# Stage B's row maxima, minima and sums move into one PSUM bank; three matmul groups share three banks; all steps in a new order

## The chip, the cores and the metric

The kernel runs on one core of a Trainium2 chip. A core has a matrix engine (PE in the profile, with its weight loads as PEld), a vector engine (DVE), a scalar engine for activations (ACT), a general engine (POOL) and a queue engine (SP) that here only starts transfers. Data is worked on in two on-chip memories: SBUF, and PSUM, into which PE writes its sums and which DVE and ACT can read and write too. This kernel cuts PSUM into eight banks of 128 partitions x 512 fp32 values. The metric is the device time of one execution in microseconds (us).

## The reference

For x with S = 2048 rows of D = 512 values, two branches are computed and mixed row by row. H = 32 heads of 16 columns, F = 1376 hidden columns, all in fp32:

```
q, k, v = x @ wqkv, cut into 32 heads of 16
pq = q @ w_phi (per head);  pk = k @ w_phi
phi(p) = concat(softmax(p), softmax(-p))       # 16 -> 32 features a head
kv = sum over rows of phi(pk)^T v;  z = sum over rows of phi(pk)
a = (phi(pq) kv) / (phi(pq) z + 1e-6) @ wo
h = x @ w1 + b1;  b = (h * tanh(softplus(h))) @ w2     # Mish
g = sigmoid(sum(x * gate_w))
out = g * a + (1 - g) * b
```

## The kernel before

Products are made to fp32 precision from two fp32r parts of each operand (high and low), as high x high + high x low + low x high. Some of the products go by a scheme of seven block products in place of eight; the steps `p1` to `p7` of a step group are these, and `c1`, `c5`, `c6`, `a2`, `a3`, `a7` (`e4` in stage A) are the additions that join them. A step is named stage, block, step: `S0.p6_2` is product 6 of pair 2 in block 0 of stage S.

- Stage A, eight chunks `A0` to `A7` of 256 rows: K and its features (`k0`, `k1`, two 128-row tiles), V and Q (`p1` to `p7`), softmaxes of K (`mx`, `mn`, `d0`, `d1`, `E`, `S`, `rS`, `ml`), products of the features with V in one PSUM bank that stays open for the whole stage (tile `kvp`), and sums of the features. The feature tile `E` (128x1024) is added into an accumulator (`zacc`, `za`) partly by transfers that POOL starts (line 484). Q is written to memory and read back as `pq` tiles of 128 rows.
- Stage S, two blocks `S0`, `S1` of 1024 rows: `x @ w1` for pairs 0 to 4 of hidden columns, into PSUM tiles `up`. ACT copies three of the seven products out (`c`), DVE adds the rest (`a2` line 740, `a3` line 743, `a7` line 746), ACT evaluates Mish (`mA`, `mB`). The weights of the next pair are made ready between: the sums `w1r` on DVE (`su`, lines 687 to 690), high parts on ACT, low parts on POOL (`w1sl`, line 700).
- Stage B, four blocks `B0` to `B3` of 512 rows: `h @ w2` in eleven steps `dn0` to `dn10` into four banks (tiles `down`), with low parts `l` made on POOL (line 824). Beside it each block makes the softmax of four `pq` tiles t = 0 to 3 on DVE: row maxima and minima of the 32 heads (`mx`, `mn`, line 275, 128x32), `E` = pq - mx and mn - pq (`d0`, `d1`, lines 285, 287), exponentials on ACT, sums `Sm` (`S`, line 291, 128x64), their reciprocals (`rS`, line 299), `T` = E * z (line 954), its sums `Dn` (`D`, line 958), the denominator (`m`, line 977: Dn * Sm; `de`, line 962), scale (`sc`, line 966), `E` scaled (`es`, line 302), transposed (`tr`, line 969) and sent through memory into `eT`. From these come `num` (`nu`), its two parts (`oh`, `ol`), `wo` and the output (`fi`).

Stages overlap: S0's first pairs run beside the end of A, the down-projection of `B0` and `B1` beside and behind S0, and so on. The order of all 1224 steps is one text, `RUN`, and every engine keeps its part of it: an instruction that waits holds all that stand behind it on the same engine, the transfers that the engine starts included. Matmuls and ACT instructions are recorded by helpers (lines 118, 138), so all of these have one line.

The eight banks are kept in three pools: `a` with three banks, `dn` with four and `kv` with one. The `kv` bank holds `kvp` in stage A. After `A7.km`, in which it is read for the last time, it serves as a fourth bank for three uses:

```
ps["a"] = psum("up", ("a", "kv")[p % 2])                          # p1 of pairs 1 and 3
po = [psum("num", tag) for tag in (("kv", "a"), ("a", "a"))[h]]
num["wo", t] = ps = psum("wo", ("kv", "a")[t % 2])
```

A new tile in a pool takes the bank whose tile is oldest, and its first matmul waits until the last reader of that tile is done. `mx`, `mn` and `Sm` of stage B are SBUF tiles, two buffers each. In stage A `S` lies in the PSUM tile of K itself (tiles `proj`), and the sources of `d0` and `d1` are PSUM tiles too.

Of the kernel before, what the change touches and what calls it, by code (L numbers as in the profile page):

```python
# [46 lines left out]
    A0.st0 A0.st1 A0.z1 A1.c6 A0.z0 A1.z0 S0.h21 A2.c1 A1.p5 A0.kv A1.c5 A1.S1 A1.rS1 A1.p7 A1.p3 A2.sh A2.sl A3.su A2.mn0 A1.ml1 A1.a7 A2.mx1 A1.st1
    A3.k1 A2.a2 A1.a3 A2.mx0 A2.d10 A2.d00 A3.p1 A2.E0 A2.S0 A3.ldx A2.rS0 A1.z1 S0.wr_0 A2.p6 A2.c6 A2.ldx A2.p5 A2.c5 A2.p7 A1.p4 A2.d01 A2.mn1
    A2.d11 A2.E1 A2.p3 A3.sh S0.wa_0 A2.ml0 A1.st0 A3.mn1 A3.c1 A3.k0 A2.a3 A2.z0 A2.st0 A3.sl A3.p5 A2.a7 A2.p4 A1.e4 A3.xh A2.S1 A3.mx0 A3.mx1
    A3.mn0 A1.kv A3.xl S0.l12 A2.e4 A2.rS1 A2.ml1 A2.kv A3.d00 A3.d10 A3.E0 S0.wb_0 S0.ws_0 A3.p6 A4.p1 A2.z1 A3.d11 A3.S0 A3.rS0 A3.ml0 A2.st1 A2.wx  # L50
    A3.c5 A4.k0 A4.mn0 A3.c6 A4.su A3.p3 A4.d10 A3.a3 A4.c1 A3.p7 A4.sh A4.mx0 S0.h11 A4.d00 A3.a7 A4.k1 A4.E0 A3.st1 A3.d01 A4.mn1 A4.d11 A4.S0 A4.sl
    A3.p2 A3.a2 A4.mx1 A4.p5 A4.p6 A3.z0 A3.E1 A4.xh A4.c6 A4.ldx A3.S1 A3.rS1 A4.p2 A4.p7 A4.d01 A4.c5 A3.ml1 A3.p4 A4.a7 A4.st1 A4.E1 A3.st0 S0.o11
    A4.xl A4.rS0 A4.ml0 A4.p3 A5.su A5.sh A4.a3 A3.z1 S0.t1 A3.e4 B0.lq0 A5.k0 A5.k1 A5.mx0 A4.S1 A4.z0 A4.rS1 A4.ml1 A5.sl S0.h1 S0.o1 A4.z1 S0.o21
    A5.xh A5.p1 A5.c1 A3.kv A5.p5 A5.c5 A4.st0 A4.a2 A5.mn0 A5.p6 A5.mx1 A5.xl A5.d01 S0.wc_0 A5.mn1 A5.d10 A5.d11 A5.d00 A5.E0 A4.p4 A5.S0 A5.rS0
# [8 lines left out]
    B0.gl B0.dn0 B0.cd B0.dn1 S0.mA1_0 S0.ws_1 S0.wc_1 A7.zf B0.d01 S0.wd_1 S0.a2_1 S0.p1_2 S0.p6_1 S0.gh3 S0.mA0_1 B0.E1 B0.hi2 B0.lo2 S0.sB0_0 A7.zs
    A7.zl B1.lq3 S0.ws_2 S0.wc_2 S0.p5_1 S0.p2_2 B0.mx2 B0.d02 S0.c6_1 S0.p7_1 S0.c5_1 S0.p3_1 S0.wr_3 B0.T1 B0.S1 B0.mn2 S0.a7_1 S0.mB1_0 S0.sB1_0
    B0.d12 B0.dn2 S0.wd_2 B0.T0 B0.hi3 B0.D1 B0.lq3 S0.c1_2 S0.p6_2 S0.mB1_1 B0.rS0 B0.E2 B0.D0 S0.wa_3 B0.lo3 S0.sB1_1 S0.a2_2 B0.rS1 B0.m1 B0.mx3
    S0.p4_1 S0.mA1_1 B0.hi4 S0.lg2 S0.c6_2 B0.de1 S0.wr_4 B0.dn3 S0.gl3 S0.wb_3 S0.mA0_2 S0.p5_2 S0.p1_3 S0.lg4 S0.c5_2 S0.a3_1 B1.lq0 S0.gh4 B0.lo4
    B0.rd1 B0.m0 B0.T2 S0.p7_2 S0.p3_2 B0.de0 S0.mB0_1 S0.ws_3 S0.wc_3 S0.wd_3 B0.sc1 S0.p2_3 B0.d03 S0.wa_4 S0.wb_4 B0.dn4 B0.es1 S0.a7_2 S0.c1_3
    S0.p6_3 S0.a3_2 B0.mn3 S0.mB0_2 S0.sB0_1 S0.a2_3 B0.d13 B1.mx3 B0.S2 S0.mB1_2 B0.D2 S0.gh2 B0.hi5 S0.c6_3 S0.mA0_3 B0.E3 S0.p4_2 B0.lo5 S0.p1_4
    S0.p5_3 S0.c5_3 B0.tr1 S0.n12 B0.rd0 B0.ge S0.gl2 B0.dn5 B0.sc0 B1.mx0 S0.ws_4 S0.p7_3 B0.es0 S0.p3_3 S0.mA1_2 S0.sB0_2 S0.a7_3 S0.p4_3 B0.rS2
    B0.hi6 S0.wc_4 B0.tr0 B0.lo6 B0.dn6 S0.mB1_3 S0.sB1_2 S0.wd_4 S0.a3_3 S0.mA1_3 S0.mB0_3 S0.sB0_3 B0.T3 B0.D3 B0.S3 B1.d00 B1.lq1 S0.gl4 B0.rS3  # L70
# [1164 lines left out]
```

## Time and profile before

| | |
|---|---|
| median of three runs | 431.92 us (431.51 to 433.22) |
| the profiled execution | 432.84 us |
| its span, first to last instruction | 431.1 us |
| PE busy | 422.3 us, 98% |
| DVE busy | 369.3 us, 86%, 519 instructions |
| ACT busy | 253.6 us, 59% |
| POOL busy | 263.6 us, 61% |
| mean granted PE clock | 0.996 of full speed |

Busy shares are means over the whole span. In a row of groups stand the line, engine and operation, output <- inputs by name, sizes, the count, and then busy time in us, mean in ns, and the idle time in front of these instructions with what ended it. In a row of the time line stand start and duration in us, and in brackets the idle time in front and what ended it. Names there lack the numbers that tell buffers apart.

### The profile page before, as it was taken

How to read it: one execution, taken by the hardware profiler on the slowest of the kernel's cores; microseconds unless marked ns; L12 is line 12 of the kernel's file. 1: busy time of each engine (PE TensorE's matmuls, PEld its weight loads, DVE VectorE, ACT ScalarE, POOL GpSimd, SP SyncE). 2: the span in 40 equal slices, each digit the busy share in tenths (PEclk: the TensorE clock that was granted, in tenths of full speed). 3: DMA queues.
4: the chain of work that ended last, by engine and by line, in shares of the span. 5: the costliest groups of instructions: out<-in, count | busy, mean ns of one | idle time of the engine just before them, and what ended most of it. 6: DMA issues, size and time to landing. Idle time of an engine off the chain costs nothing. (4 is left out here: it accounts for less than half of the span.)

```text
span 431.1 us, 7558 instructions
## 1 busy us (share of the span) xinstructions
PE 422.3 (98%) x2772; PEld 340.2 (79%) x2772; DVE 369.3 (86%) x519; ACT 253.6 (59%) x373; POOL 263.6 (61%) x186
## 2 busy tenths in 40 slices
PE   8999999999998999899999999999999999999996
PEld 7888888888886877688878687788788887877875
DVE  3899789998998999998999998799989699999512
ACT  3574463646254899768679813467978467851131
POOL 2298868799674966635666494977455627541220
PEclk9999999999999999989999999999999999999999
DMA  7900597675988344433888477833533725555532
GB/s 260 366 34 28 164 273 182 140 179 126 209 171 214 108 134 123 160 109 122 235 249 281 165 239 237 281 91 122 177 119 143 232 73 188 179 199 168 197 121 75
DMA packets 52670, 74.06 MB, mean 172 GB/s; under 512 B 8085, under 2 KB 32149, under 8 KB 52633
## 3 DMA queue, kind: packets, MB, share of 16 engines
q1 hardware_dynamic: 50440, 66.36, 47.9%
q0 software_dynamic: 1904, 6.82, 9.5%
q8 instruction: 22, 0.36, 0.3%
q10 hardware_dynamic: 288, 0.39, 0.3%
q14 instruction: 16, 0.12, 0.1%
HBM read 43.53 MB, written 28.85 MB: 168 GB/s over the span
## 5 line engine op out<-in xcount | busy, mean ns | idle before, releaser
L118 PE MATMUL down<-w2g,h 128*128 128x512 f32 x316 | 98.5, 393 | 0.0
L118 PEld LDWEIGHTS down<-w2g,h 128*128 128x128 f32 x316 | 58.6, 188 | 14.8 <-issue 2.5
L118 PE MATMUL down<-w2g,l 128*128 128x512 f32 x158 | 61.8, 391 | 0.2 <-POOL l L824 0.2
L824 POOL TENSOR_TENSOR l<-act,h 128x512 fp32r<-128x512 f32 (+1 forms) x24 | 32.3, 1345 | 41.2 <-ACT h L138 16.7
L824 POOL TENSOR_TENSOR l<-actb,h 128x512 fp32r<-128x512 f32 x20 | 29.0, 1451 | 38.3 <-ACT h L138 20.7
L138 ACT ACTIVATE E<-E 128x1024 f32<-128x1024 f32 x32 | 33.4, 1057 | 16.5 <-DVE E L285 7.1
L118 PE MATMUL up<-x,w1sh 128*128 128x512 f32 x144 | 39.7, 397 | 2.2 <-DVE act L740 2.1
L118 PE MATMUL wo<-woh,ohl 128*128 128x512 f32 x128 | 40.9, 389 | 0.0
L118 PEld LDWEIGHTS down<-w2g,l 128*128 128x128 f32 x158 | 29.6, 188 | 7.5 <-POOL l L824 1.2
L118 PEld LDWEIGHTS up<-x,w1sh 128*128 128x128 f32 x144 | 26.7, 189 | 9.2 <-DVE act L740 2.5
L700 POOL TENSOR_TENSOR w1sl<-w1r,w1sh 128x1024 fp32r<-128x1024 f32 x9 | 22.2, 2467 | 18.0 <-ACT w1sh L138 17.4
L118 PE MATMUL proj<-tw,sx 128*128 128x512 f32 x126 | 31.5, 394 | 1.5 <-ACT qs L138 1.5
L628 POOL TENSOR_TENSOR x<-xr,x 128x1024 fp32r<-128x1024 f32 x10 | 26.7, 2666 | 3.6 <-ACT x L138 3.6
L118 PEld LDWEIGHTS proj<-tw,sx 128*128 128x128 f32 x126 | 23.3, 188 | 6.9 <-ACT qs L138 1.9
L138 ACT ACT_TABLE_LOAD x22 | 28.2, 1283 | 0.4
L118 PEld LDWEIGHTS wo<-woh,ohl 128*128 128x128 f32 x128 | 24.0, 188 | 5.0
L138 ACT ACTIVATE act<-act,b1s 128x512 f32<-128x512 f32 x30 | 21.4, 719 | 10.9 <-DVE act L740 4.1
L118 PE MATMUL up<-x,w1d 128*128 128x512 f32 x108 | 27.7, 398 | 0.0
L267 POOL TENSOR_TENSOR xl<-xraw,xh 128x512 fp32r<-128x512 f32 x14 | 18.3, 1370 | 15.3 <-ACT xh L138 15.0
L138 ACT ACTIVATE act<-up 128x512 f32<-128x512 f32 x30 | 17.6, 590 | 16.8 <-PE up L118 16.4
L138 ACT ACTIVATE h<-actb 128x512 fp32r<-128x512 f32 x20 | 12.4, 628 | 24.4 <-DMA actb<-ab 18.9
L118 PE MATMUL wo<-wol,ohl 128*128 128x512 f32 x64 | 24.9, 389 | 0.0
(173 smaller groups left out, 1086.4 us busy)
## 6 DMA issues: line engine op xcount, KB each, us to landing
ed<-E SPq DMA_DIRECT2D x16, 512.0 KB, 3.1
eT<-ed SPq DMA_DIRECT2D x64, 128.0 KB, 3.2
za<-E POOLq DMA_DIRECT2D x11, 512.0 KB, 6.8
xr<-in_xT_dram SPq DMA_DIRECT2D x20, 256.0 KB, 4.2
ab<-act SPq DMA_DIRECT2D x20, 256.0 KB, 2.9
actb<-ab SPq DMA_DIRECT2D x20, 256.0 KB, 3.3
pqd<-qs SPq DMA_DIRECT2D x16, 256.0 KB, 5.8
pq<-pqd SPq DMA_DIRECT2D x16, 256.0 KB, 3.6
```

The lines of the kernel that those rows point to most:

```text
L118: return pin(nc.tensor.matmul(*a, **k))
L138: return pin(A_.activation(out_, in_, fn, **k))
L267: pin(eng.tensor_sub(xs[c][1][j], kt(rawx[c], SC)[:, 2 * j : 2 * j + 2, :], f32(xs[c][0][j])))
L628: pin((V if n in LOV else G_).tensor_sub(X[n][:, 1024:], xr[n], f32(X[n][:, :1024])))
L700: pin(G_.tensor_sub(W["sl"], W["r"], f32(W["sh"])))
L824: pin(G_.tensor_sub(U[i]["l"][:n, :], U[i]["a"][:n, :], f32(U[i]["h"][:n, :])))
```

## The change

Behind `A7.km` the `kv` bank becomes one tile `sm` that stays to the end. It is cut into three slots of 160 columns. A stage B softmax tile takes a slot, if one is free, at the first of its `mx` and `mn`, keeps `mx`, `mn`, `Sm` and a new product `m` in it, and gives it back at its `es`; if none is free, it uses SBUF tiles as before. By the order of the steps ten of the sixteen tiles get a slot: t = 2, 3 of B0, t = 0, 2, 3 of B1, t = 1, 2, 3 of B2 and t = 1, 2 of B3. For these, `m` is two multiplications of 128x32, the second into the slot, in place of one of 128x64, which adds ten DVE instructions. `up`, `num` and `wo` take the three `a` banks alone. `RUN` is written anew. The matmuls are the same in number. ACT loads its tables 21 times in the program's order, where it was 23.

```diff
 RUN = """
-    A0.mx0 A0.mx1 A0.xh A0.xl A0.v0 A0.mn1 A0.mn0 A0.fq A0.fh2 S0.l11 A0.d10 A0.tA0 A0.fh1 A0.v1 A0.tA1 A0.tH1 A0.fl1 A0.tB1 A0.tB0 A0.fl2 A1.p1
...
+    A1.ldx A0.mn1 A0.v1 A0.d11 A0.xh A0.mn0 A0.xl A0.ve1 A0.d10 A0.mx1 A0.fq A0.fh0 A0.fh2 A0.tA0 S0.l11 A0.d01 A0.tA1 A0.tH1 A0.mx0 A0.fh3 A0.fl3
 """
...
+    B = {}
+    sm, slots = [], [0, 1, 2]
+
+    def small(d, name, o, n, bufs=2):
+        if "slot" not in d:
+            d["slot"] = None
+            if slots and "km" in B:
+                if not sm:
+                    sm.append(psum("sm", "kv"))
+                d["slot"] = slots.pop(0)
+        if d["slot"] is None:
+            return T([P, n], F32, name, bufs, name)
+        o += 160 * d["slot"]
+        return sm[0][:, o : o + n]
...
-            d[name] = T([P, H], F32, name, 2, name)
+            d[name] = small(d, name, H * (name == "mn"), H) if key[0] == "B" else T([P, H], F32, name, 2, name)
...
-            d["S"] = src()[:, : 2 * H] if key[0] == "A" and key[1] else T([P, 2 * H], F32, "Sm", 2, "Sm")
+            if key[0] == "B":
+                d["S"] = small(d, "Sm", 2 * H, 2 * H)
+            else:
+                d["S"] = src()[:, : 2 * H] if key[1] else T([P, 2 * H], F32, "Sm", 2, "Sm")
...
-                ps["a"] = psum("up", ("a", "kv")[p % 2])
+                ps["a"] = psum("up", "a")
...
+            def dm(d=d):
+                if d["slot"] is None:
+                    d["m"] = d["D"][:, H:]
+                    pin(V.tensor_mul(d["D"], d["D"], d["S"]))
+                    return
+                d["m"] = small(d, "", 4 * H, H)
+                pin(V.tensor_mul(d["D"][:, :H], d["D"][:, :H], d["S"][:, :H]))
+                pin(V.tensor_mul(d["m"], d["D"][:, H:], d["S"][:, H:]))
...
-                pin(V.scalar_tensor_tensor(d["d"], d["D"][:, :H], 1e-6, d["D"][:, H:], op0=ALU.add, op1=ALU.add))
+                pin(V.scalar_tensor_tensor(d["d"], d["D"][:, :H], 1e-6, d["m"], op0=ALU.add, op1=ALU.add))
+
+            def es(d=d):
+                scale_by(d, V)
+                if d["slot"] is not None:
+                    slots.append(d["slot"])
...
-                po = [psum("num", tag) for tag in (("kv", "a"), ("a", "a"))[h]]
+                po = [psum("num", "a") for _ in range(2)]
...
-                num["wo", t] = ps = psum("wo", ("kv", "a")[t % 2])
+                num["wo", t] = ps = psum("wo", "a")
```

New line numbers stand some 15 to 30 higher: lines 285, 287, 291, 302 become 301, 303, 310, 321; 687 to 690 become 706 to 709; 740, 743, 746 become 759, 762, 765; 954, 958, 977 become 971, 975 and 980 to 984.

Three places show the order. The first is PE in block 0 of stage S, between pairs 2 and 3; `w1sh`, `w1sl`, `w1d`, `w1o` are weight parts, the number behind a name tells tiles apart. Before:

```order
L118 MATMUL up_1902<-x_595,w1o_1774 128x512 x6
L118 MATMUL up_1787<-x_1570,w1sh_1850 128x512 x4
...
L118 MATMUL up_1787<-x_1634,w1d_1671 128x512 x6
...
L118 MATMUL down_1825<-w2g_211_1561,l_1984 128x512
L118 MATMUL up_2031<-x_1105,w1sh_1893 128x512 x4
L118 MATMUL up_2031<-x_1105,w1sl_1956 128x512 x2
L118 MATMUL up_2038<-x_960,w1d_1980 128x512 x6
L118 MATMUL up_1861<-x_1570,w1sh_1893 128x512 x4
```

`up_2031` (`S0.p5_2`) takes the bank of `up_1902`, whose last matmul lies 48 matmuls of 512 columns back. Now, at the same pairs:

```order
L118 MATMUL up_2003<-x_1083,w1sl_1985 128x512 x2
L118 MATMUL up_2010<-x_1081,w1o_1975 128x512 x6
...
L118 MATMUL down_1784<-w2g_200_1503,l_2019 128x512
L118 MATMUL up_2003<-x_1469,w1sh_1937 128x512 x4
L118 MATMUL up_2003<-x_1469,w1sl_1985 128x512 x2
L118 MATMUL up_1941<-x_1629,w1sh_1937 128x512 x4
L118 MATMUL up_1941<-x_1629,w1sl_1985 128x512 x2
L118 MATMUL up_2079<-x_543,w1d_1974 128x512 x6
```

`up_2079` (`S0.p1_3`) takes the bank of `up_2003`, whose last matmul lies six matmuls back. `up_2010` is `S0.p2_3`.

The second is DVE at that place; `act` are Mish inputs, `w1r` weight sums, `den` denominators. Before:

```order
L285 TENSOR_TENSOR E_1911<-pq_1739,mx_1909 128x512
L954 TENSOR_TENSOR T_1933<-E_1527,zb_1885 128x1024
L291 TENSOR_REDUCE Sm_1935<-E_1527 128x64
L275 TENSOR_REDUCE mn_1937<-pq_1739 128x32
L746 SCALAR_TENSOR_TENSOR act_1921<-up_1787,act_1921 128x512
L287 TENSOR_TENSOR E_1911<-mn_1937,pq_1739 128x512
L954 TENSOR_TENSOR T_1958<-E_1527,zb_1885 128x1024
L958 TENSOR_REDUCE Dn_1962<-T_1933 128x64
L299 RECIPROCAL Sm_1813<-Sm_1813 128x64
L958 TENSOR_REDUCE Dn_1978<-T_1958 128x64
L740 TENSOR_TENSOR act_1966<-up_1902,act_1966 128x512
```

The last row, `S0.a2_2`, reads `up_1902` and so lets `up_2031` begin. Now:

```order
L759 TENSOR_TENSOR act_1948<-up_1895,act_1948 128x512
L318 RECIPROCAL Sm_1876<-Sm_1876 128x64
L971 TENSOR_TENSOR T_1993<-E_1605,zb_1964 128x1024
L975 TENSOR_REDUCE Dn_2021<-T_1993 128x64
L980 TENSOR_TENSOR Dn_2021<-Dn_2021,Sm_1876 128x64
L971 TENSOR_TENSOR T_2024<-E_1605,zb_1964 128x1024
...
L706 TENSOR_TENSOR w1r_1923<-w1r_1923 128x2x128
...
L310 TENSOR_REDUCE sm_1880<-E_1886 128x64
L762 TENSOR_TENSOR act_2063<-up_2003,act_2063 128x512
L765 SCALAR_TENSOR_TENSOR act_2055<-up_1941,act_2055 128x512
```

The rows from `T_1993` to `sm_1880` now stand between `S0.a2_2` (line 759), which lets `up_2010` begin, and `S0.a3_2` (lines 762, 765), which lets `up_2079` begin.

The third is POOL where stage A ends and S0 begins; `xl`, `sx` and `x` are low parts of inputs, `w1f` and `w1sl` of weights. Before:

```order
L267 TENSOR_TENSOR xl_1275<-xraw_1270,xh_1273 128x512
L360 TENSOR_TENSOR xraw_1270<-xraw_1270 128x2x128 x4
L484 DMA za_125<-E_1296 128x1024
L368 TENSOR_TENSOR sx_523<-xraw_1270,sx_523 128x1024
L484 DMA zacc_124<-E_1296 128x1024
L790 TENSOR_TENSOR w1f_1426<-w1r_1392,w1f_1425 128x512
L628 TENSOR_TENSOR x_1442<-xr_1337,x_1442 128x1024
```

Now:

```order
L503 DMA za_125<-E_1298 128x1024
L379 TENSOR_TENSOR xraw_1283<-xraw_1283 128x2x128 x4
L387 TENSOR_TENSOR sx_559<-xraw_1283,sx_559 128x1024
L647 TENSOR_TENSOR x_1469<-xr_1347,x_1469 128x1024
L503 DMA zacc_124<-E_1298 128x1024
L578 TENSOR_TENSOR w2g_200_1503<-raw_1445,w2g_200_1503 128x512
L578 TENSOR_TENSOR w2g_200_1503<-raw_1447,w2g_200_1503 128x512
L809 TENSOR_TENSOR w1f_1520<-w1r_1515,w1f_1519 128x512
```

`x` now stands ahead of the last transfer from `E` into `zacc`, and `x` and two `w2g` parts stand ahead of `w1f`.

More of the change, by code (lines that the diff above doesn't have):

```diff
@@ L47 @@
[L47 to L54, printed above, removed]
@@ L63 @@
[L63 to L70, printed above, removed]
@@ L87 @@
-    B2.dn1 S1.wr_4 B2.m0 S1.wr_3 S1.ws_2 S1.c1_2 S1.a7_1 B2.hi2 B2.d13 S1.p2_2 S1.a2_2 B3.mn0 S1.mB1_1 S1.sB1_1 B2.de0 B2.lo2 S1.wc_2 S1.wd_2 B2.dn2
-    B2.E3 S1.p4_1 S1.wa_3 S1.wb_3 S1.p5_2 S1.c5_2 B2.T3 B2.D3 B3.mx1 S1.p6_2 B2.hi3 B2.lo3 S1.p3_2 S1.c6_2 S1.p7_2 B3.lq3 S1.a3_1 S1.mB0_1 B3.mx3
-    B2.rd0 B2.sc0 B2.sc1 S1.mA1_1 S1.a3_2 B2.dn3 S1.n12 S1.p2_3 B3.mn1 S1.ws_3 S1.mB0_2 B2.hi4 S1.a7_2 S1.mB1_2 S1.p4_2 S1.sB0_2 B2.es0 B2.tr0
-    S1.sB1_2 S1.p1_3 B2.lo4 B2.dn4 S1.wa_4 S1.wb_4 B2.S2 S1.p2_4 S1.sB0_1 B2.es1 S1.mA0_2 B2.hi5 B2.tr1 B2.mv0 S1.wc_3 B2.S3 S1.c1_3 S1.a2_3 S1.mA0_3
@@ new lines @@
+    B0.mx3 B0.d03 S0.ws_2 S0.gh2 S0.p2_2 A7.zs S0.p3_1 S0.c6_1 S0.a3_1 S0.gl2 S0.p7_1 B0.mn2 B0.mx2 B0.d02 S0.wr_3 S0.lg4 S0.a7_1 B0.hi2 B0.lo2 B0.E1
+    S0.wc_2 B0.S1 S0.p1_2 S0.c1_2 B0.dn2 B1.mn0 B0.d13 A7.zl B0.d12 S0.p4_1 B0.rS1 S0.wa_3 S0.a2_2 S0.mB1_1 S0.sB1_1 B0.rS0 B1.lq3 S0.wd_2 S0.p6_2
+    B0.T0 S0.mB0_1 S0.sB0_1 S0.wb_3 S0.mA1_1 S0.mA0_1 S0.p5_2 S0.p2_3 B0.hi3 B0.lo3 B0.D0 B0.m0 B0.T1 B0.de0 S0.mA0_2 S0.ws_3 B0.dn3 B0.rd0 S0.sB1_0
+    B0.E3 B0.S3 S0.wr_4 B0.hi4 S0.c5_2 S0.p3_2 S0.c6_2 B0.lo4 S0.wc_3 S0.a3_2 S0.p7_2 B0.E2 S0.a7_2 B0.S2 S0.p1_3 B0.sc0 S0.wd_3 B0.dn4 S0.lg3 B0.es0
@@ new lines @@
+    S1.c6_0 S1.ws_1 S1.wc_1 B2.T3 B2.D3 S1.wd_1 S1.p2_0 S1.a2_0 S1.h4 B2.lo0 S1.wr_2 B1.fi0 S1.p3_0 S1.a3_0 B2.gl B2.S1 B2.rS1 S1.p7_0 S1.p5_1 B2.hc
+    S1.mA0_0 B1.df1 B1.fi2 S1.p1_1 S1.c5_1 S1.o4 S1.c1_1 S1.p3_1 B2.T1 S1.p6_1 B1.fi1 S1.c6_1 S1.a3_1 B2.dn0 S1.wa_2 S1.wb_2 B2.hi1 B2.D1 S1.p7_1
+    S1.a7_1 S1.a7_0 S1.mB0_1 S1.p2_1 B2.cd B2.lo1 B2.m1 S1.a2_1 S1.p4_0 S1.mA1_0 S1.sB0_1 B2.dn1 S1.mB0_0 S1.p1_2 S1.ws_2 S1.wr_4 B2.de1 S1.p4_1
+    B2.hi2 S1.wc_2 S1.mA0_1 S1.sB0_0 B2.rd1 S1.p2_2 B2.lo2 B2.dn2 S1.mB1_1 B2.T0 B2.D0 B2.S3 S1.wr_3 B2.S0 B2.rS0 B2.m0 S1.wd_2 B2.hi3 S1.c1_2 S1.a2_2
@@ new lines @@
+    B2.d02 B2.E2 B3.mx3 S1.sB1_1 S1.n12 S1.wa_3 B2.lo3 S1.mB1_0 S1.p6_2 S1.c6_2 B2.dn3 S1.wb_3 S1.p5_2 S1.mA0_2 S1.sB1_0 S1.ws_3 B2.rS3 B2.m3 S1.mA1_1
+    B2.hi4 S1.p7_2 S1.c5_2 S1.p3_2 B2.sc1 B2.es1 B2.lo4 B2.de0 S1.wc_3 B3.mn3 S1.p2_3 S1.wa_4 S1.a3_2 B2.hi5 S1.mB0_2 S1.p1_3 S1.sB0_2 B3.lq0 S1.a7_2
+    S1.mB1_2 B2.tr1 S1.c1_3 S1.a2_3 S1.mA0_3 S1.wd_3 B2.dn4 B2.lo5 B2.S2 S1.p5_3 S1.p4_2 S1.sB1_2 B2.rd0 B2.sc0 B2.es0 S1.c5_3 S1.p6_3 S1.c6_3 B2.de3
+    B2.tr0 S1.wb_4 S1.p3_3 S1.p7_3 B2.rd3 B2.sc3 S1.mA1_2 B2.hi6 S1.ws_4 S1.a7_3 B2.lo6 B3.mn1 S1.p1_4 S1.p4_3 B2.dn5 S1.wc_4 S1.wd_4 B2.hi7 B2.lo7
@@ L103 @@
+    B3.la6 B3.hi8 B3.tr2 B3.ol0 B3.dn4 B3.dn5 B3.rS3 B3.m3 B3.de3 B3.rd3 B3.wo0 B3.la9 B3.la10 B3.hi6 B3.sc3 B3.lo6 B3.dn6 B3.ag0 B3.hi9 B3.es3 B3.tr3
+    B3.mv1 B3.hi7 B3.lo7 B3.lo8 B3.wo1 B3.dn7 B3.dn8 B3.hi10 B3.lo9 B3.ag1 B3.nu1 B2.fi3 B3.oh1 B3.ol1 B3.lo10 B3.df1 B3.wo3 B3.ag3 B3.df0 B3.fi1
+    B3.wo2 B3.fi0 B3.ag2 B3.df2 B3.fi2 B3.fi3
 """
@@ L980, in b_ops @@
             at(key, f"sc{t}", sc)
-            at(key, f"es{t}", lambda d=d: scale_by(d, V))
+            at(key, f"es{t}", es)
             at(key, f"tr{t}", tr)
```

86 lines of the change are left out of this document (45 added, 41 removed).

## The prediction

> **What bounds the kernel.** The first lines of the page say how much each engine works.
>
> ```profile
> span 431.1 us, 7558 instructions
> PE 422.3 (98%) x2772; PEld 340.2 (79%) x2772; DVE 369.3 (86%) x519; ACT 253.6 (59%) x373; POOL 263.6 (61%) x186
> ```
>
> PE is the bound, and the change leaves its matmuls as they are. Time can come only from PE's idle time and from matmuls that ran slowly. So I read next PE's waits (engine, what for, us in total, times, longest), and then stretches of the span (length, busy time of PE, PEld, DVE, ACT and POOL, granted clock, DMA share, GB/s).
>
> ```profile
> PE up L118 <- DVE act L740: 2.1, 1, 2.1
> PE proj L118 <- ACT qs L138: 1.5, 1, 1.5
> PE warm L118 <- DVE ones L188: 1.1, 1, 1.1
> PE up L118 <- POOL w1sl L700: 0.3, 1, 0.3
> PE proj L118 <- DVE wkh L1094: 0.2, 1, 0.2
> PE down L118 <- POOL l L824: 0.2, 1, 0.2
> ```
>
> ```profile
> 135.00:250.00 115.00, 110.99 (x592) 87.78 (x591) 107.65 (x154) 90.41 (x130) 72.96 (x46) 0.99 0.58 175
> 176.00:182.40 6.40, 4.41 (x20) 3.32 (x18) 6.40 (x7) 6.31 (x9) 4.43 (x5) 1.00 0.43 152
> 182.40:185.80 3.40, 3.31 (x9) 2.64 (x10) 3.37 (x9) 1.32 (x2) 0.93 (x1) 0.60 0.86 262
> 185.80:190.00 4.20, 4.20 (x19) 3.39 (x18) 4.04 (x10) 2.67 (x4) 0.00 (x0) 0.92 0.17 60
> ```
>
> The stretch from 135 to 250 us holds nearly all idle time behind the start. The wait of 2.1 us for line 740 ends at 182.49. In the 3.4 us behind it the granted clock is 0.60, in the next 4.2 us 0.92: 0.40 x 3.4 + 0.08 x 4.2 = 1.7 us more. The start's 1.1 us isn't touched. So the most that any new order can win back is 2.1 + 1.7 + 1.5 + 0.3 + 0.2 + 0.2 = 6.0 us; a little of it always stays, and I count 5.8. The time line shows how the 2.1 us came about.
>
> ```profile
> 168.06 1.57 DVE L285 TENSOR_TENSOR E<-pq,mx 128x512 f32<-128x512 f32 x1
> 169.55 3.43 DVE L954 TENSOR_TENSOR T<-E,zb 128x1024 f32<-128x1024 f32 x1
> 175.10 3.00 POOL L559 TENSOR_TENSOR w2g<-raw,w2g 128x512 fp32r<-128x512 f32 x2
> 175.22 1.72 DVE L287 TENSOR_TENSOR E<-mn,pq 128x512 f32<-128x512 f32 x1
> 176.86 2.31 DVE L954 TENSOR_TENSOR T<-E,zb 128x1024 f32<-128x1024 f32 x1
> 181.77 0.67 DVE L740 TENSOR_TENSOR act<-up,act 128x512 f32<-128x512 f32 x1
> 182.49 1.62 PE L118 MATMUL up<-x,w1sh 128*128 128x512 f32 x4 [2.08 <-DVE act L740]
> ```
>
> DVE was never idle here, but four instructions took longer than usual. The instructions on tile `E` show what usual is (count, then shortest, median and longest in ns, first and last start).
>
> ```profile
> L287 DVE TENSOR_TENSOR E<-mn,proj x16: 670/678/689, 17.3 to 136.7; 128x512 f32<-128x512 f32 x16
> L285 DVE TENSOR_TENSOR E<-proj,mx x16: 673/681/692, 24.6 to 136.1; 128x512 f32<-128x512 f32 x16
> L285 DVE TENSOR_TENSOR E<-pq,mx x16: 639/685/2882, 131.5 to 383.1; 128x512 f32<-128x512 f32 x16
> L287 DVE TENSOR_TENSOR E<-mn,pq x16: 622/690/2179, 149.1 to 383.7; 128x512 f32<-128x512 f32 x16
> L954 DVE TENSOR_TENSOR T<-E,zb x16: 1160/1218/3426, 169.5 to 388.3; 128x1024 f32<-128x1024 f32 x16
> ```
>
> The same subtraction with one input in PSUM (`proj`, stage A) never takes over 692 ns. With both in SBUF (stage B) it takes up to 2882. The long ones run beside POOL, as at 175.10.
>
> **The change, part by part.** Durations come from the groups of line and form (busy us, mean ns | idle).
>
> ```profile
> L285 DVE TENSOR_TENSOR E<-pq,mx 128x512 f32<-128x512 f32 x16 | 15.8, 986 | 0.1
> L287 DVE TENSOR_TENSOR E<-mn,pq 128x512 f32<-128x512 f32 x16 | 18.5, 1158 | 0.1
> L977 DVE TENSOR_TENSOR Dn<-Dn,Sm 128x64 f32<-128x64 f32 x16 | 7.7, 482 | 0.3
> L962 DVE SCALAR_TENSOR_TENSOR den<-Dn 128x32 f32<-128x32 f32 x16 | 4.2, 267 | 0.2
> L299 DVE RECIPROCAL Sm<-Sm 128x64 f32<-128x64 f32 x18 | 9.6, 538 | 0.1
> L299 DVE RECIPROCAL proj<-proj 128x64 f32<-128x64 f32 x14 | 7.8, 558 | 0.3
> ```
>
> *Small tiles in PSUM.* Ten tiles have `d0` and `d1` with one PSUM input, which should take 682 and 678 ns: 10 x ((986 - 682) + (1158 - 678)) = 7.8 us less DVE work. The split `m` adds ten instructions: nearly nothing if two halves cost as one, 10 x 0.48 = 4.8 us if each costs as much as the whole; the nearest row of 32 columns is line 962 with 267 ns, two of which exceed 482 by 0.05, so I take 1 us with the PSUM writes. Reading small tiles from PSUM costs next to nothing by the two reciprocals: 20 ns. DVE then ends near 369.3 - 7.8 + 1 = 362.5 us. Off PE's path that is worth nothing. In the stretch that stalled, before 190 us, only two or three tiles with slots are worked on, since B0.t0 and t1 have none: there the gain is about 2 us.
>
> [...]
>
> *The unprotected work.* `T` (line 954) has both inputs in SBUF still, and so have the sums `w1r`.
>
> ```profile
> L954 DVE TENSOR_TENSOR T<-E,zb 128x1024 f32<-128x1024 f32 x16 | 23.7, 1489 | 0.8 <-ACT E L138 0.8
> L687 DVE TENSOR_TENSOR w1r<-w1r 128x256 f32<-128x256 f32 x10 | 6.3, 630 | 0.0
> L690 DVE TENSOR_TENSOR w1r<-w1r 128x256 f32<-128x256 f32 x10 | 4.3, 426 | 1.0 <-DVE w1r L689 0.2
> L743 DVE TENSOR_TENSOR act<-up,act 128x512 f32<-128x512 f32 x10 | 6.8, 677 | 0.4 <-issue 0.3
> L958 DVE TENSOR_REDUCE Dn<-T 128x64 f32<-128x1024 f32 x16 | 19.2, 1200 | 0.2
> ```
>
> *Three banks in place of four.* A matmul of 512 columns takes 227 ns:
>
> ```profile
> 312.57 2.72 PE down L118 x12
> ```
>
> In the old order the closest reuse of an `up` bank that waits for another tile's reader has 12 matmuls between, 2.72 us. In the new one seven such places have six or fewer, 1.36 us. The reader needs 0.68 us (line 743), and with the last matmul's own end about 0.9 us, if its engine is free at once. The slack is 0.45 us, and DVE is busy 86% of the time with pieces of 0.5 to 1.5 us.
>
> The longest of the seven is `S0.p1_3`, behind the order shown. From `S0.a2_2`'s end DVE does a reciprocal 0.54, `T` 1.49, `Dn` 1.20, `m` 0.48, `T` 1.49, `den` 0.27, four `w1r` near 2.0 (lines 687 to 690), a reciprocal (under 0.54, say 0.3), `S` about 1.2 (as `Dn`) and `a3` 0.68: 9.6 us. PE has from `S0.p2_3`, which waits for `a2_2`, 30 matmuls: 6.8 us. So `p1_3` waits 2.8 us if `a2_2` comes just in time, and nothing if DVE is 2.8 us ahead there. I take 1.2, nearer to nothing, since that stretch begins with three protected subtractions. The other six lie between nothing and 0.75 us each (a 1.2 us piece in front, less the slack): 0 to 4.5, taken as 1.5, as only some meet a long piece.
>
> *A to S.* POOL's queue now has `x` and two `w2g` parts in front of `w1f`, and `x` in front of the last transfer out of `E`.
>
> ```profile
> L628 POOL TENSOR_TENSOR x<-xr,x 128x1024 fp32r<-128x1024 f32 x10 | 26.7, 2666 | 3.6 <-ACT x L138 3.6
> zacc<-E POOLq DMA_DIRECT2D x1, 512.0 KB, 5.1
> ```
>
> The transfer starts up to 2.67 us later, and takes 5.1. DVE's next `d1` writes that `E` buffer and must wait for it; behind it in DVE's queue stand the K softmax of A7 and with it a bank that an early S0 product takes. Cost 0 to 2.7 us, taken as 1.0. `w1f` stands behind 2.67 + 3.00 us of POOL work that was elsewhere; POOL is idle 39% of the time, so between 0 and 5.7, taken as 1.2 with the wait of A7's product 6 for `sx` on the same queue.
>
> *Start.* `A1.p1` now stands so early that its bank is still held by the fused weights, which `wqh` and `wql` read.
>
> ```profile
> 23.40 1.07 ACT L138 ACTIVATE wqh<-fuse 128x512 fp32r<-128x512 f32 x2
> 24.01 0.69 DVE L1167 TENSOR_TENSOR wql<-fuse,wqh 128x512 fp32r<-128x512 f32 x1 [0.42 <-ACT wqh L138]
> ```
>
> By these and the new rows ahead, PE is there at about 24.2 and `wql` ends at about 25.1: 1.0 us, between nothing and 2.
>
> *Covered.* Two table loads fewer on ACT lie beside PE, as ACT works 59% of the time. The same four `down` banks and the same transfers on SP carry stage B; The closest reuses of `num` and `wo` have six matmuls between, once in the old order and twice in the new one; if that cover fails, it costs one more 0.75 at most, which the other six places' range takes in.
>
> *The sum.* -5.8 + 1.0 (start) + 1.0 + 1.2 (A to S) + 1.2 (`p1_3`) + 1.5 (other banks) = +0.1 us. The profiled execution took 432.84 us for a span of 431.1, so 1.7 lie around it, and 0.9 above the median of 431.92. I predict 432.0 in terms of the median. A change within 0.5%, 2.16 us, can't be told from none.
>
> **Rivals.**
>
> *The relief is real and the banks fit.* For it: in the old order handoffs of 1.4 us inside one tile, by an ACT copy, mostly cost nothing, and DVE has 7 us less to do. Against it: the relief is small before 190 us. Lost are then the start and one or two short waits, 2.0 us: 431.9 - 5.8 + 2.0 = 428.1; with 3 us lost, 429.1.
>
> *Slower: a three-bank handoff meets a blocked `T`.* The place is `S0.p1_3`, or its like in pairs 2 and 4. A `T` of 3.43 in place of 1.49 adds 1.9 us to the 1.2 there: 3.1 us of idle PE. The old trace shows that 2.1 us idle brought the clock to 0.60, 1.7 us more, while the 1.5 us wait did not. The point from which it decides is thus an idle time of about 2 us. Two such places cost 2 x (3.1 + 1.7) = 9.6 in place of the 1.2 and 0.7 counted: 432.0 + 7.7 = 439.7; one costs 4.8 - 1.2 = 3.6: 435.6. Against it: each needs POOL's long instruction to start just before `T`.
>
> *Slower by the clock alone.* Many waits under 1 us, one at each handoff, could lower the clock with no long stall: six places at 1.7 us each are 10.2 us, 442. The stretch after the 1.5 us wait kept a clock of 1.00 in the old trace, hence a chance of 0.03. [...]
>
> *The change doesn't do what it says.* POOL's reads could block `T` and `w1r` more, once `d0` and `d1` no longer take the blows: DVE stays at 367 to 369 us, and the first estimate loses nothing but the 2 us of relief: up to 434.
>
> **How the numbers follow.** The forecast, a trade of one stall for several short waits, has 0.39 within 0.5%. Relief that fits: 0.25, faster. The blocked handoff: 0.25, of it nearly all slower by over 0.5%. The clock alone 0.03, slower. Blocked work that moves to `T`: 0.08, two thirds of it slower. So 0.27 faster (0.02 from the forecast's own spread), 0.38 same, 0.35 slower. The forecast's own range is 430 to 434. The range for 8 in 10 runs from 428.4, with the first rival's values but the lowest, to 437.5, one blocked handoff and half of another; both ends leave out about 1 in 10.
>
> **What would show it.** `d0` and `d1` of the ten tiles at or below 692 ns, with maxima over 2000 left only among the other six; the wait for DVE's `a2` gone or below 1 us; in its place waits of `up` for DVE `act` (lines 759 to 765) and of `proj` for `wql` near 24 us, each about 1 us; DVE busy near 362. The prediction is wrong if PE waits less than 3 us in all behind the start with the clock at 1.00 (then about 428), or if a stretch behind one of the seven handoffs has a clock near 0.6 (then 435 and more).

## The result, and the profile after

The changed kernel takes 432.93 us in the median of 18 runs (431.04 to 436.41); the old one, run beside it, 430.69 us (426.35 to 434.11). The ratio is 1.0069, with a 95% interval of 1.0040 to 1.0098: slower by 0.7%. The ratio leaves out the old kernel's three longest runs, 432.80 to 434.11 us, as runs of a slower state; over all 36 runs the means differ by 0.56%. A repeat (e4 below) gave 1.0035 (1.0003 to 1.0067). So the change costs about half a per cent. Runs of the old kernel on their own spread over 8 us, which turns out to matter: two of the 18 lie near 426.5 us, the others at 429.3 to 434.1.

The first lines of the page after, and PE's waits:

```profile
span 431.5 us, 7571 instructions
PE 423.7 (98%) x2772; PEld 340.3 (79%) x2772; DVE 357.9 (83%) x529; ACT 250.7 (58%) x371; POOL 255.3 (59%) x186
```

```profile
PE num L118 <- ACT gr L138: 1.5, 1, 1.5
PE warm L118 <- DVE ones L188: 1.1, 1, 1.1
PE wo L118 <- DVE ohl L1043: 0.6, 1, 0.6
PE up L118 <- DVE act L759: 0.3, 1, 0.3
PE up L118 <- POOL w1e L719: 0.3, 1, 0.3
PE proj L118 <- DVE wql L1198: 0.2, 1, 0.2
PE up L118 <- DVE act L762: 0.2, 1, 0.2
```

The waits of 2.1 us (`a2`) and 1.5 us (`qs`) are gone. In their place stand one of 1.5 us near 378 us and several of 0.2 to 0.6. Outside the start they add up to 3.1 us, where it was 4.3. In the stretches of the span, the idle PE with a lowered clock behind it, which stood at 182 us in the old trace, now stands at 378 (PE waits from 377.55 to 379.04, and the half clock lasts from 379.06 to 382.47):

```profile
135.00:250.00 115.00, 114.82 (x677) 91.75 (x676) 105.34 (x161) 85.97 (x129) 74.28 (x49) 1.00 0.59 182
376.90:378.40 1.50, 0.65 (x6) 0.13 (x2) 1.50 (x2) 0.00 (x0) 1.47 (x1) 1.00 0.00 0
378.40:381.80 3.40, 2.76 (x32) 1.44 (x33) 1.11 (x2) 3.37 (x4) 0.00 (x0) 0.60 0.49 165
381.80:386.00 4.20, 4.20 (x18) 3.38 (x18) 3.63 (x5) 3.36 (x6) 0.00 (x0) 0.92 0.48 131
```

The time line there shows who held `num`:

```profile
374.75 3.62 POOL L843 TENSOR_TENSOR l<-actb,h 128x512 fp32r<-128x512 f32 x2 [2.49 <-ACT h L138]
378.40 0.59 ACT L138 ACTIVATE gr<-up 1x512 f32<-1x512 f32 x1 [3.21 <-POOL l L843]
379.04 1.96 PE L118 MATMUL num<-eT,kvb 64*32 64x256 f32 x30 [1.50 <-ACT gr L138]
```

`B3.gr` copies one row out of an `up` bank. ACT could not start it, because POOL's `l` ended only at 378.37, and gave its buffer free only then. The second half of B2's `num` takes the bank that `gr` reads, and waited with it.

The instructions on tile `E` of DVE are as the change intends (`sm` is the new PSUM tile):

```profile
L301 DVE TENSOR_TENSOR E<-pq,sm x10: 626/682/687, 164.3 to 378.8; 128x512 f32<-128x512 f32 x10
L303 DVE TENSOR_TENSOR E<-sm,pq x10: 680/691/692, 173.6 to 372.5; 128x512 f32<-128x512 f32 x10
L303 DVE TENSOR_TENSOR E<-mn,pq x6: 646/1002/1609, 138.5 to 376.6; 128x512 f32<-128x512 f32 x6
L301 DVE TENSOR_TENSOR E<-pq,mx x6: 649/684/1752, 139.9 to 377.2; 128x512 f32<-128x512 f32 x6
L971 DVE TENSOR_TENSOR T<-E,zb x16: 1159/1217/1841, 176.2 to 385.9; 128x1024 f32<-128x1024 f32 x16
```

None of the twenty protected subtractions takes over 692 ns; among the other twelve some still reach 1.6 to 1.75 us. DVE's busy time fell by 11.4 us, and the kernel is not faster.

### The profile page after: what moved, and what is told of

Its sections match the earlier page's. It is cut to its first block, busy times and chain, and to the rows that moved or that the text cites. A ratio compares the mean times of both kernels' runs of the same rounds, so it can differ in the third digit from the quotient of the medians.

```text
span 431.5 us, 7571 instructions
## 1 busy us (share of the span) xinstructions
PE 423.7 (98%) x2772; PEld 340.3 (79%) x2772; DVE 357.9 (83%) x529; ACT 250.7 (58%) x371; POOL 255.3 (59%) x186
## 4 chain that ended last, share of the span: by engine, by line
PE 76%; DVE 13%; DMA 3%; issue 3%; ACT 3%; POOL 1%; SPq 1%; DVEq 0%; POOLq 0%; ACTq 0%
PE proj L118 25%; PE up L118 22%; PE down L118 19%; PE wo L118 6%; DMA xraw<-in_xT_dram 2%; PE kvp L118 2%; DVE T L971 1%; PE num L118 1%; DVE E L321 1%; DVE Dn L975 1%; DVE E L1000 1%; DMA bds<-in_bd_dram 1%; DVE ohl L1043 1%; POOL l L843 1%; DVE sm L291 1%
## 5 line engine op out<-in xcount | busy, mean ns | idle before, releaser
L118 PE MATMUL up<-x,w1sh 128*128 128x512 f32 x144 | 38.7, 391 | 0.3 <-DVE act L759 0.3
L647 POOL TENSOR_TENSOR x<-xr,x 128x1024 fp32r<-128x1024 f32 x10 | 25.7, 2600 | 3.7 <-ACT x L138 3.7
L379 POOL TENSOR_TENSOR xraw<-xraw 128x256 f32<-128x256 f32 x28 | 23.9, 853 | 1.7
```

Source lines behind the costliest of these rows:

```text
L118: return pin(nc.tensor.matmul(*a, **k))
L379: pin(G_.tensor_add(o, o, i))
L647: pin((V if n in LOV else G_).tensor_sub(X[n][:, 1024:], xr[n], f32(X[n][:, :1024])))
```

## The experiments

The line numbers of the experiments stand up to five higher than those of the kernel they come from.

**What the PSUM tiles are worth in the new order: e1, e5, e6, e11.** e1 takes the slots away:

```diff
-    sm, slots = [], [0, 1, 2]
+    sm, slots = [], []
```

with `Sm` and `mn` in three buffers, `den` in one, `ge` and `g` in one tile and `B0.S2` moved behind `B0.es0`, since the new order keeps more small tiles alive than two buffers hold. e5 makes these adjustments, but for the third buffers, and keeps the slots. e6 puts `mx` and `mn` in SBUF and leaves `Sm` and `m` in PSUM; e11 does the reverse on top of e5, with `m` in one instruction again.

> The new order with the small tiles of stage B all in SBUF; up, num and wo keep three banks, and the eighth bank stays unused. One step (B0.S2) stands a little later and a few small tiles have one buffer more or less, so that all fit. Theory P (the PSUM tiles keep DVE off PE's path): the subtractions of lines 285 and 287 take up to 2000 ns and more again, DVE is busy 8 to 12 us longer than in the changed kernel's 357.9 us, PE waits for the additions of up at least 2 us longer in all, and the time is 2 to 5 us above the changed kernel, a ratio to the old kernel of 1.012 to 1.018. Theory O (DVE's longer work lies beside PE in the new order): DVE is longer in the same way, but PE's waits and the time stay within 1 us of the changed kernel, a ratio of 1.005 to 1.009.

> The changed kernel with only the small adjustments that e1 needed (B0.S2 a little later, one buffer for den, ge and g in one tile), and the small tiles in PSUM. If e1's 20 us come from SBUF tiles, this stays within 1 us of the changed kernel (430.5 to 433.5). If they come from the adjustments, it lies above 440.

> The changed kernel with mx and mn in SBUF (mn with three buffers), Sm and m in the PSUM slots. The subtractions of lines 285 and 287 are then exposed to POOL again, the scaling of E (line 302) is not. Theory D (the subtractions carry the relief): most of e1's loss, 10 to 18 us, comes back, with up's waits for DVE. Theory S (the scaling of E by Sm carries it, which the prediction left out): under 5 us comes back, and line 302 stays near 1211 ns where e1 had 1468.

> The counterpart of e6, on the adjustments of e5: mx and mn in the PSUM slots, Sm and m in SBUF, and m in one instruction. If the losses of e1 (19 us over e5) add up, this costs e1's less e6's, about 11 us: 442 to 444, with line 302 near 1468 ns. If e1's loss is more than the sum, since blocked subtractions and blocked scalings lie one behind the other on DVE, it costs less than 8 us: under 440.

| | small tiles in PSUM | median us | ratio to the old kernel (95%) | DVE busy us |
|---|---|---|---|---|
| e5 | all | 432.33 | 1.0036 (0.9999 to 1.0073) | 359.3 |
| e6 | `Sm`, `m` | 440.83 | 1.0187 (1.0131 to 1.0242) | 366.0 |
| e11 | `mx`, `mn` | 445.32 | 1.0295 (1.0251 to 1.0339) | 370.2 |
| e1 | none | 451.68 | 1.0463 (1.0415 to 1.0511) | 379.6 |

The adjustments cost nothing that shows (e5). The PSUM tiles are worth 4.3% in the new order by the ratios of e1 and e5, some 18 us, and 20 us by the medians of e1 and e4, which ran on the same chip; that is far above what either theory named for e1. Against e5, e6 loses 1.5%, e11 2.6%, together 4.1%: within intervals of about half a per cent each way, the parts add up. By the medians e6 lies 8.5 us above e5, between the ranges of its two theories (under 5, and 10 to 18), so neither of them holds as it was put. The five largest of PE's waits in e1, and the group of `E`'s scaling in e1 and in e5:

```profile
PE down L120 <- POOL l L845: 2.8, 4, 1.2
PE up L120 <- DVE act L764: 2.7, 1, 2.7
PE num L120 <- ACT gr L140: 2.1, 1, 2.1
PE up L120 <- DVE act L767: 1.7, 1, 1.7
PE wo L120 <- DVE ohl L1045: 1.4, 1, 1.4
```

```profile
L323 DVE TENSOR_TENSOR E<-E,Sm 128x1024 f32<-128x1024 f32 x18 | 26.4, 1468 | 0.4
```

```profile
L323 DVE TENSOR_TENSOR E<-E,sm 128x1024 f32<-128x1024 f32 x10 | 12.1, 1211 | 0.2
```

With `Sm` in SBUF the scaling has two SBUF inputs too, and takes 1468 ns on average; with `sm` in PSUM 1211. I had not counted this instruction among the protected ones at all. By e6 and e11 the tiles `Sm` and `m` carry the larger part of the gain; how much of that is the scaling is not shown, and of the 10.9 us that DVE works longer in e11 than in e5 it takes 4.0. The counterpart, the PSUM tiles in the old order, was not run: that order keeps four `up` tiles alive at once, and the bank is not free. In e6 the largest wait is this one:

```profile
PE up L118 <- DVE act L767: 2.7, 1, 2.7
```

It is `S0.p1_3`'s wait for `a3`, from 186.7 to 189.3 us.

**A bank back: e2.** e1, and `num` and `wo` with the eighth bank again:

```diff
-                po = [psum("num", "a") for _ in range(2)]
+                po = [psum("num", tag) for tag in (("kv", "a"), ("a", "a"))[h]]
-                num["wo", t] = ps = psum("wo", "a")
+                num["wo", t] = ps = psum("wo", ("kv", "a")[t % 2])
```

> As e1, and the eighth bank is given back to num and wo as in the old kernel (the first of num's tiles and wo's even ones); up keeps three banks. Theory B (a bank too few is what the new kernel pays for): the wait of num for ACT's gr (1.5 us in the changed kernel) and that of wo for DVE's ohl (0.6) are gone, and the time lies 2 to 4 us below e1. Rival (the banks of num and wo cost nothing by themselves): within 1 us of e1, since the second half of num took two of the three banks in the old kernel too.

The six runs lie in two groups, two at 448.9 and four at 456 to 460; the ratio of the lower ones is 1.0402 (1.0324 to 1.0481), an interval that holds e1's 1.0463. The profile is of the upper group, and has a wait that e1 has not:

```profile
PE num L120 <- DVE io L1094: 8.8, 1, 8.8
```

`num` waits 8.8 us for the one bank until `fi` has read the `wo` that lies in it. Neither theory expected that, and whether the two lower runs have it is not shown. The theory of the missing bank stays open: the two lower runs lie 2.8 us below e1, as it has it, but the other four lie 4 to 8 us above, and `num`'s wait for `gr`, which it said would go, is still 2.1 us in the profile. So what the lost bank costs by itself was not separated.

**One late copy: e3, with e4 beside it.** e4 is the changed kernel again; e3 moves one step.

```diff
-    B3.d12 B3.rd0 B3.hi2 B3.lo2 B3.hi1 B3.dn0 B2.fi0 B3.sc0 B3.cd B3.es0 B3.lo1 B3.gr
+    B3.d12 B3.gr B3.rd0 B3.hi2 B3.lo2 B3.hi1 B3.dn0 B2.fi0 B3.sc0 B3.cd B3.es0 B3.lo1
```

> The changed kernel with one step moved: B3.gr, ACT's copy of the gate row out of an up bank, stands two high parts earlier, where it waits for no POOL instruction. Theory G (the time of the changed kernel is set by num's wait for gr and the lowered clock behind it): num's wait falls from 1.5 us to under 0.3, no stretch near 378 us has a lowered clock, fewer of the runs have a mean clock below 0.997, and the time falls by 1.5 to 3.2 us, a ratio to the old kernel of 0.999 to 1.003. Rival (the loss is spread over the order): the wait goes, but another of the same size takes its place within 50 us, and the ratio stays 1.005 to 1.009.

> The changed kernel unaltered, on the same chip as e1 to e3, as their measure. Both theories: a ratio to the old kernel of 1.004 to 1.010, and two groups of runs: near 431.5 us where the mean clock is 0.999 or more, near 434 us where it is 0.995, since one window of 3.41 us at half clock costs 1.7 us and the wait of num comes with it.

e3 takes 430.60 us (ratio 1.0023, 0.9987 to 1.0058), e4 431.65 (1.0035, 1.0003 to 1.0067). Behind the start's 1.1 us, the three largest of PE's waits in e3, and the two largest in e4:

```profile
PE down L120 <- POOL l L845: 0.6, 1, 0.6
PE proj L120 <- DVE wql L1200: 0.5, 1, 0.5
PE wo L120 <- DVE ohl L1045: 0.4, 1, 0.4
```

```profile
PE down L118 <- POOL l L843: 2.2, 2, 1.8
PE num L118 <- ACT gr L138: 1.5, 1, 1.5
```

`num`'s wait is gone, and nothing of that size replaces it. The time falls by 1.05 us, less than expected, and the intervals overlap; theory G has the place right, but most of the runs of e4 had no lowered clock to lose: nine of twelve have a mean clock of 0.998 or more, though the same wait of 1.5 us stands in its profile. The group near 434 us that was expected of e4 did not come: its three runs with a mean clock of 0.995 take 432.2 to 433.0.

**Two more places: e7.** e3, and steps of S1 and A0 moved:

```diff
-    A0.fh2 A0.tA0 S0.l11 A0.d01 A0.tA1 A0.tH1 A0.mx0 A0.fh3 A0.fl3 A0.v0 A0.fl2 A0.fh1
+    A0.fh2 A0.fh3 A0.fh1 A0.tA0 S0.l11 A0.d01 A0.tA1 A0.tH1 A0.mx0 A0.fl3 A0.v0 A0.fl2
...
-    S1.h22 S1.h1 B1.sc2 B1.lo7 B1.m3 B1.de3 B1.rd3 S1.o1 B1.dn7 B1.es2 B1.tr2 B1.hi8 B1.lo8 B0.fi1 B1.sc3 B1.hi9
+    B1.sc2 B1.lo7 B1.m3 B1.de3 B1.rd3 B1.dn7 B1.es2 B1.tr2 B1.hi8 B1.lo8 B0.fi1 B1.sc3 B1.hi9 S1.h22 S1.h1 S1.o1
```

> e3 with two more places mended: two ACT conversions of x for S1 that waited 8.3 us for a transfer, ahead of a high part that B1's down-projection needs, stand behind it; and two wqh parts stand ahead of the first tw, so that A1.p1 finds its bank free. Theory (the changed kernel's loss is five or six short waits, each with its own cause): the wait of down for POOL's l near 258 us (0.6 in e3, 1.8 in the changed kernel's repeat) and of proj for wql (0.5 to 0.8) go below 0.2, and the time falls by 1 to 1.5 us below e3, to 429.0 to 429.7, a ratio to the old kernel below 1.0. Rival (waits only move on): no change against e3, 430.6.

437.02 us, ratio 1.0113 (1.0063 to 1.0163), 0.9% above e3 by the ratios. PE's waits:

```profile
PE proj L120 <- ACT qs L140: 2.1, 1, 2.1
PE down L120 <- POOL l L845: 1.8, 1, 1.8
PE wo L120 <- DVE ohl L1045: 1.5, 2, 1.1
```

The wait for `wql` is gone, the wait for `l` near 260 us is still 1.8, and a new wait for `qs` ends at 49.7 us. The time line ahead of it shows DVE's scaling of `E` starting 0.19 us behind POOL's `sx`:

```profile
41.15 2.40 POOL L389 TENSOR_TENSOR sx<-xraw,sx 128x1024 fp32r<-128x1024 f32 x1 [1.17 <-ACT sx L140]
41.34 3.29 DVE L323 TENSOR_TENSOR E<-E,Sm 128x1024 f32<-128x1024 f32 x1
```

The same scaling took 1.22 us in e3. DVE's last instruction on `twr`, at 31.80 us, took 3.40 us beside POOL's `tw`, where e3 has 1.22. Behind the two DVE stands 3.2 us later than in e3; ACT's exponential waits for it until 47.06, and `qs` comes behind that. POOL's last `tw` itself ends 0.3 us earlier than in e3. The rival, that waits move on, holds, and more: two small repairs cost more than they mended.

**The old kernel's own spread: e8, e9, e10, e12.**

> The old kernel unaltered, for a second profile. Of its earlier runs a third had a mean clock of 0.999 or more and a median of 427.9 us, the others 0.995 or 0.996 and 430 to 434. If the stall at 182 us is fixed by the order, it is here again with about 2 us. If it hangs on how DVE's and POOL's instructions meet in each execution, its length is another, and in a run near 427 us it is below 1 us and the clock stays at 1.00.

This execution took 426.45 us with a span of 424.7. PE's waits are down to two:

```profile
PE warm L118 <- DVE ones L188: 1.1, 1, 1.1
PE proj L118 <- DVE wkh L1094: 0.2, 1, 0.2
```

The same kernel, the same order, and both large waits are gone. It is no rare outcome: of the 75 runs of the old kernel beside e1 to e12, 19 lie below 429 us, all with a mean clock of 0.999 or 1.000 (which runs of 430 to 434 us can have too). None of the changed kernel's 30 runs, e4 included, lies below 430.97. The time line of this execution, at the place that stalled in the first profile:

```profile
166.92 1.21 DVE L954 TENSOR_TENSOR T<-E,zb 128x1024 f32<-128x1024 f32 x1
167.21 3.21 POOL L700 TENSOR_TENSOR w1sl<-w1r,w1sh 128x1024 fp32r<-128x1024 f32 x1 [0.76 <-PE up L118]
174.78 0.67 DVE L740 TENSOR_TENSOR act<-up,act 128x512 f32<-128x512 f32 x1
```

And in the first profile of the old kernel, the row that belongs to its `T` of 3.43 us at 169.55:

```profile
169.39 2.50 POOL L700 TENSOR_TENSOR w1sl<-w1r,w1sh 128x1024 fp32r<-128x1024 f32 x1 [0.31 <-PE up L118]
```

Where `T` starts 0.29 us ahead of `w1sl`, `T` takes 1.21 us and POOL's instruction 3.21. Where it starts 0.16 us behind, `T` takes 3.43 and POOL's 2.50. In both, the one that comes first takes about what it takes elsewhere: 1.21 us where the median of `T` in e8 is 1.22, 2.50 where the median of `w1sl` in the first profile is 2.41. From this `T` on, the addition of line 740 falls 4.4 us further behind in the first profile than in e8: 2.2 us at this `T`, and 1.0 and 1.1 at the `d1` and the second `T`, which then run into POOL's `w2g` at 175.10. By these traces the stall hangs on less than half a microsecond; no run changes that half microsecond alone.

e9 moves `S0.a2_2` ahead of the second `T`. e10 is e9 with `S0.gh1` and `S0.gl1` behind `A7.c6`. e12 leaves both as they were, moves `A6.zm`, a transfer of 512 KB, behind `S0.gl1`, and `A7.z0` beside `A7.z1`.

```diff
-    B0.T0 B0.hi3 B0.D1 B0.lq3 S0.c1_2
+    B0.hi3 B0.lq3 S0.c1_2 S0.a2_2 B0.T0 B0.D1
```

> The old kernel with one piece of DVE's queue turned round: S0.a2_2 (line 740), for which PE waited 2.1 us, stands ahead of the second T and its sums instead of behind them. Small tiles and banks as in the old kernel. Theory L (the old kernel's runs above 430 us come from PE waiting there when POOL blocks T, and the lowered clock behind it): the wait is gone whatever T takes, most runs have a mean clock of 0.998 or more, and the median falls from 430 to 432 to 427 to 428.5 us, a ratio of 0.990 to 0.995. Rival (other waits lower the clock too): fewer than half of the runs change, a ratio above 0.997.

> e9, and the two ACT conversions of w2g that once held ACT's qs for a late transfer (PE waited 1.5 us at 140 us) stand behind that qs. If that wait is common in the runs of the old kernel, this falls a further 0.5 to 1.5 us below e9; if it is rare, it equals e9 within 0.5 us.

> The old kernel with two POOL steps moved: A6.zm, the 512 KB transfer of za onto zacc, stands behind the low parts of w2g that ACT's late w2g conversion feeds, and the first addition into zacc (A7.z0) stands beside the second. Theory Z (the old kernel's spread begins where the transfers of w2a and of zacc meet: where w2a comes late, ACT, PE and DVE are shifted by 1.5 us, T then meets POOL's w1sl and is blocked, and PE waits again with a lowered clock): ACT's wait for w2a (4.1 us) falls below 1, PE's waits for qs and for line 740 are gone, most runs lie at 426 to 428.5 us, a ratio of 0.988 to 0.995. Rival (the lateness has another cause, or POOL's later additions hold B0's softmax): the wait for w2a stays in the profile or another takes its place, a ratio above 0.997.

e9: 430.63 us, ratio 0.9993 (0.9959 to 1.0027). e10: 434.00, 1.0065 (1.0037 to 1.0093). e12: 430.95, 1.0010 (0.9973 to 1.0047). None is faster than the old kernel. So theory L fails: with the wait for line 740 gone the median stays, and that wait alone is not what holds most runs of the old kernel above 430 us. In e9 the wait for line 742 (the old 740) is gone, but `T` is blocked as before (3.43 us, started 0.17 us behind `w1sl`), and PE waits elsewhere:

```profile
PE proj L120 <- ACT qs L140: 1.4, 1, 1.4
PE up L120 <- ACT act L140: 0.8, 2, 0.6
PE up L120 <- POOL w1sl L702: 0.7, 2, 0.5
```

In e10 the 1.5 us wait for `qs` is still there, now because ACT's `qs` waits for its own buffer's transfer (4.73 us), and three waits for `w1sl` add 3.8 us. In e12 ACT's wait for `w2a` falls from 4.12 to 0.44 us and the wait for `qs` is gone, as theory Z has it; but `T` is blocked all the same, and PE waits for line 742 (the old 740) as in the first profile:

```profile
PE up L120 <- DVE act L742: 2.1, 1, 2.1
```

```profile
167.99 2.50 POOL L702 TENSOR_TENSOR w1sl<-w1r,w1sh 128x1024 fp32r<-128x1024 f32 x1 [0.32 <-PE up L120]
168.14 3.43 DVE L956 TENSOR_TENSOR T<-E,zb 128x1024 f32<-128x1024 f32 x1
```

So the 1.5 us wait goes with transfers that come late (in e10 it is another one), but they are not what decides between `T` and `w1sl`. What decides which of the two starts first stays open.

## Why the prediction was right or wrong

The forecast, 432.0 us, is 0.9 us off the measured 432.93, and the range held it. By ratio the forecast of no change, within 0.5%, failed narrowly in the first comparison (0.7% slower, 0.56% over all runs) and held in the repeat (0.35%). The working behind it was right in its bound and wrong in several terms that cancelled, so that the sum came this close is in part luck.

*What can be won back: 5.8 of 6.0 us.* The size was right: e8's span is 431.1 - 424.7 = 6.4 us shorter. What failed is the reading of it as a fixed loss of the old order. The profile showed one outcome of several, and in some of its runs the old kernel wins the 6 us by itself. Its median beside the changed kernel was 430.69, not 431.92, and that is where the 0.7% begins. A single run's profile can't tell a fixed wait from one that comes and goes. The rows of `E` and `T`, with shortest and longest a factor of three and more apart, only say that instructions are blocked. In e8, without the stall, they are as far apart:

```profile
L954 DVE TENSOR_TENSOR T<-E,zb x16: 1159/1216/3459, 166.9 to 381.8; 128x1024 f32<-128x1024 f32 x16
```

*The relief.* `d0` and `d1` gained 10 x ((986 - 673) + (1158 - 688)) = 7.8 us by the groups of both traces, as forecast; against e8, whose two means are 992 and 962, it is 5.9 us. DVE fell by 11.4 us against the first profile and by 6.7 against e8, where 7 was forecast, so part of the fall belongs to that one execution. The term for the small instructions was wrong: the split `m` with `den` takes 182 + 195 + 184 = 561 ns a tile, not 1 us in all above the old 749 but 188 ns below it. `T`'s mean fell to 1245 ns, from 1489 in the first profile and 1422 in e8. The rival that blocked time would merely move to `T` is refuted, and so is the step "off PE's path that is worth nothing". By e1 the new order leans on those tiles with 18 to 20 us.

*`S0.p1_3`: 1.2 us of 0 to 2.8.* PE waited 0.2 us (line 762). The place is right: with `mx` and `mn` in SBUF (e6) it is the largest wait, 2.7 us, close to the upper bound of 2.8. The sum of DVE's queue there was about right too: from `a2_2`'s end to `a3`'s it takes 9.0 us where 9.6 were forecast. What I misjudged is how far ahead DVE is: PE reaches `p2_3` at 177.72, 1.9 us behind `a2_2`'s end.

*A to S: 2.2 us.* Nothing: between 135 and 250 us PE is busy for 114.82 of 115.

*Start: 1.0 us.* The place and cause are right (`wql`); 0.2 us in this execution, 0.5 to 0.8 in those of e3, e4 and e5.

*Other banks: 1.5 us.* In size too small, since `num` (1.5), `wo` (0.6) and `up` (0.3) together make 2.4; in mechanism only half right. I had looked for DVE or ACT being late for a bank. The largest, `num`, waits for a bank whose reader on ACT was held by another buffer, in SBUF, that POOL still read. That chain of bank, buffer and third engine was not in the working: it took `num` and `wo` as covered, at 0.75 us at most if the cover fails, and they cost 2.1.

*The clock.* The point "about 2 us" failed: 1.5 us lowered the clock in this execution, 1.7 us more, and not in e4 and e5; 2.1 us did not in e7, whose mean clock of 0.998 leaves no room for 1.7 us (that would be 0.996). The rival of the blocked `T` did not come: `T`'s longest is 1841 ns. The rival of the clock alone did not either: where no such wait stands (e3), the mean clock of most runs is 0.999 or 1.000 with three banks in use.

Set against the first profile: 4.3 us of waits and 1.7 of lowered clock before, 3.1 and 1.7 after, which would be 1.2 us shorter; the span is 0.4 longer. PE's busy time rose by 1.4 us, part of it at the start, where the full clock came 1.4 us later in this execution (at 7.00 us, in the first profile at 5.56); the rest is not settled. One sign of being wrong was less than 3 us of waits behind the start with the clock at 1.00, then about 428 us. e3's profiled execution has just that, 2.3 us and 1.00, and took 430.47: some 2.4 us of the new order's cost lie outside PE's waits, and where is open.

## What to carry to other kernels

When one profile shows a stall, look at the shortest and longest duration of the instructions ahead of it: if they are far apart, as with `T` here (1.16 to 3.43 us with the stall, 1.16 to 3.46 in e8 without it), take a second profile, for the stall may be there in one execution and not in the next. Look at buffers and order together: the whole change gained nothing, while its PSUM tiles alone are worth 18 to 20 us within the order that came with them. When a bank is taken away, follow each reader of it through its own queue and its own output buffer, up to the third engine.
